# Attention scores in one group of 512 columns a head, left-over keys on the whole array, scores kept in DRAM

## The chip, the core and the metric

The kernel runs on one core of a Trainium2 chip. A core has five engines that run side by side, each taking its own instructions in order: TensorE (PE; its weight loads are the row PEld), VectorE (DVE), ScalarE (ACT), GpSimd (POOL) and SyncE (SP, which here only issues DMAs). TensorE writes PSUM, eight banks of 2 KB a partition; everything else works on SBUF. The metric is the device time of one execution in microseconds. Of the kernel before there are three timed runs and one profiled execution.

## The reference

Attention that keeps the 32 largest scores of each row, then a mixture of experts in which each token goes to one expert. Batch 8, 8 heads, 576 positions, head size 64; 4608 tokens of 512 features, 8 experts with 1024 hidden units; all fp32.

```python
scores = scale * np.matmul(q, k.transpose(0, 1, 3, 2))
kth = np.partition(scores, -top_k, axis=-1)[..., -top_k:-top_k + 1]
scores = np.where(scores >= kth, scores, -1000000000.0)
attn = np.exp(scores - np.max(scores, axis=-1, keepdims=True))
attn = attn / (np.sum(attn, axis=-1, keepdims=True) + 1e-09)
x = np.matmul(attn, v)                       # then (token, head * 64)
logits = x @ w_gate
expert_idx = np.argmax(logits, axis=1)       # one expert a token
out[mask] = gate_w[mask, None] * (np.maximum(x[mask] @ w1[e], 0.0) @ w2[e])
```

## The kernel before, in words

**Tiles and steps.** A head has 576 = 4 x 128 + 64 rows: four main tiles of 128 rows (`MAIN`) and 64 left-over rows (`LEFT`). Two heads make a pair `p`; batch `b` has four pairs. The attention runs in 144 steps, nine for each two pairs (`NT` = 9), so eighteen for a batch. A step (`grp(t)`, L333) takes two tiles, tile i of the first and of the second head of a pair; one step in nine takes the left-over rows of two pairs instead. So a step has 2 x 128 rows of 576 scores, kept side by side in one `sb` buffer of 2 x 576 columns (`EX[t]`, seven buffers), in the order main keys of the first, left-over keys of the first, left-over keys of the second, main keys of the second.

**One pass of the loop (L962).** Every engine's part of a step lies some passes behind the step before it in the chain. In pass t the program issues:

- scores of step t+3 (`scores`, L347) in two halves. A half is two matmuls of 288 columns, one a head, with 64 rows of weights each, so that the two lie in the two halves of the array; they write `ps` (two banks, one buffer), and `evac` (L366) copies 2 x 288 columns out on ACT. The second half uses the same `ps`. The first half stands at the start of the pass, the second after `av`.
- `softmax` of step t-2 (L397): for each of the two tiles ACT writes the sign of score minus threshold into `sg` and counts it, and POOL adds that to `sb` in place (L409).
- `exps` of step t-4 (L428): ACT takes exp of `tt`, the 1152 turned columns in PSUM, into `et`.
- `av` of step t-5 (L432): the left-over keys by a full-array matmul (L454), the main keys by 16 half-width instructions (L439), into `px`.
- `transp` of step t-3 (L411): subtracts the row maximum by four bf16 matmuls (L422) and turns `sb` by nine transposes (L425) into `tt`.
- top-k of step t (`topk`, L373) on VectorE: 21 MAX8 over chunks of the scores, then MAX8 and MATCH_REPLACE8 over the candidates.

**Jobs.** Smaller work runs between the steps as generators. `advance` (L850) moves each on when its banks are free and the pass's limits allow it; what it issues goes into queues `pq`, `aq`, `dq`, `gq` that are flushed at fixed places of the pass (`pq` stands between the first half of the scores and `av`). `j_prep` turns q and k of a pair. The turned k (`kt`, twelve buffers) stays until its batch is done. `j_sums` and `j_rows` make row sums and write finished rows to DRAM (`xs`, `lps`). `j_find`, `j_redo`, `j_patch` mend up to 128 rows of a batch whose count of kept scores isn't 32: `j_find` fetches their q rows from DRAM, spreads them by head (`qx`, 512 columns) and turns them; `j_redo` forms their scores anew against the turned k of all heads, 2 x 4 matmuls of 288 columns, and finds the exact threshold; `j_patch` writes the mended rows. `j_route` gives each token its place. Loads of the next q and k (`load_qk`, L99) and v (L270) are issued on SP at fixed steps, and wait until the one buffer of `rq` or `rk` has been read.

**PSUM.** `tt` has three banks, of which the columns from 1152 on (`SPOTS`) serve small results of jobs; `ps` has two, `px` one, and two banks (`pt`) go round among the jobs.

**After the attention**, the experts: for each of eight blocks of hidden units of an expert, `hidden` (L1102) and `project` (L1117) in split fp32r; the change doesn't touch them. The first experts' work begins while the last batches' jobs end.

Of the kernel before, what the change touches and what calls it, by code (L numbers as in the profile page):

```python
# [47 lines left out]
def attention_moe(ctx, tc, q, k, v, w_gate, w1, w2, out):  # L48
# [50 lines left out]
    def load_qk(n):  # L99
# [3 lines left out]
        lq = work.tile([LEFT, 4, D], F32, name="lq", bufs=1)  # L103
        lk = work.tile([LEFT, 4, D], F32, name="lk", bufs=1)
        LD[n] = (rq, rk, lq, lk)

        for g in ((slice(0, 2), slice(2, 4)) if n == 0 else (slice(0, 4),)):
            hs = slice(4 * hf + g.start, 4 * hf + g.stop)
            for t, src, l, eng in ((rq, q, lq, nc.sync), (rk, k, lk, nc.sync if n or g.start else nc.scalar)):
# [133 lines left out]
    VV, KT, SB, EX, ET, XT, PX = {}, {}, {}, [], {}, {}, {}  # L243
# [44 lines left out]
    three = psum.tile([128, 3 * 512], F32, name="tt")  # L288


    SPOTS = dict(left=(0, 128), stat=(128, 8), li=(136, 8), logit=(144, 16), rank=(160, KB * E))

    def spot(name):
        if not att_open[0]:
            pt = bank()
            return pt, lambda: release(pt)
        o, w = SPOTS[name]
        held[0] += 1

        def leave():  # L300
            held[0] -= 1
            cell[0] += name == "left"
        return three[:, NB9 * 128 + o:NB9 * 128 + o + w], leave

    def j_prep(p):
        rq, rk, lq, lk = LD[p // 2]
        qt = QT[p % 3]
        hs = slice(2 * (p % 2), 2 * (p % 2) + 2)
        yield need(bank=1, pe=0.5, act=0.5)
        KT[p] = jobs.tile([128, KW], F32, name="kt", bufs=12)  # L310
        for r, d, o in ((rq, qt, 2 * LEFT), (rk, KT[p], LEFT)):
# [16 lines left out]
        act(nc.scalar.activation, kl, pt[:, None, LEFT:2 * LEFT].to_broadcast([128, 2, LEFT]), AF.Copy)
# [16 lines left out]
    EV = []  # L345

    def scores(slot, hf):  # L347
# [3 lines left out]
        if hf == 0:  # L351
            EX.append(pair())
# [1084 lines left out]
```

## Time and profile before

| | |
|---|---|
| median of 3 runs | 1362.01 us (1361.56 to 1364.34) |
| the profiled execution's own time | 1361.72 us |
| its span, first to last instruction | 1359.9 us |
| mean granted TensorE clock | 0.990 |
| busy, share of the span | PE 97%, DVE 76%, ACT 62%, POOL 67% |
| attention (steps and most jobs) | from about 7 to about 842 us |
| instructions | 32355 |
| DMA packets, bytes | 207878, 124.17 MB |

How to read the rows: in a timeline row stand the start in us, the length in us, engine, line, operation, output<-input tiles, partitions x columns, and the count of instructions merged into the row; a bracket tells the idle time before it and what ended it. A matmul's length is its way through the array, so the time from one start to the next tells what it costs in a row of matmuls. In a windows row stand the stretch, its length, each engine's busy time with its instructions, the granted clock, the DMA engines' busy share and GB/s. In a row of groups stand shape, count, busy us and mean ns. In a row of waits stand who waited for whom, us in total, times and the longest. fp32 matmuls run as two instructions each, transposes as one. L252 is the line of the helper that all jobs go through, so jobs are told apart by tile.

### The profile page before, as it was taken

How to read it: one execution, taken by the hardware profiler on the slowest of the kernel's cores; microseconds unless marked ns; L12 is line 12 of the kernel's file. 1: busy time of each engine (PE TensorE's matmuls, PEld its weight loads, DVE VectorE, ACT ScalarE, POOL GpSimd, SP SyncE). 2: the span in 40 equal slices, each digit the busy share in tenths (PEclk: the TensorE clock that was granted, in tenths of full speed). 3: DMA queues.
4: the chain of work that ended last, by engine and by line, in shares of the span. 5: the costliest groups of instructions: out<-in, count | busy, mean ns of one | idle time of the engine just before them, and what ended most of it. 6: DMA issues, size and time to landing. Idle time of an engine off the chain costs nothing.

```text
span 1359.9 us, 32355 instructions
## 1 busy us (share of the span) xinstructions
PE 1318.6 (97%) x10072; PEld 1037.0 (76%) x10072; DVE 1026.9 (76%) x6838; ACT 841.1 (62%) x1715; POOL 906.9 (67%) x1280
## 2 busy tenths in 40 slices
PE   6899999999999999999999998999999999999997
PEld 3667777777777777777777676888889899898996
DVE  7989998899999899999999795564674333345664
ACT  4888888788788789688788675333333233233432
POOL 4676877777787787787787797747654232355664
PEclk7999999999999999999999999999999999999999
DMA  4211312212212211221221022554665333346774
GB/s 117 56 37 42 77 36 57 61 42 58 61 41 57 62 42 50 59 51 42 61 57 42 16 63 69 158 171 136 187 174 158 97 124 94 112 139 185 218 217 127
DMA packets 207878, 124.17 MB, mean 91 GB/s; under 512 B 110104, under 2 KB 188104, under 8 KB 207696
## 3 DMA queue, kind: packets, MB, share of 16 engines
q1 hardware_dynamic: 197344, 100.95, 27.9%
q0 software_dynamic: 9120, 20.76, 4.9%
q8 instruction: 81, 1.33, 0.4%
q14 instruction: 101, 0.83, 0.2%
q10 hardware_dynamic: 1232, 0.30, 0.1%
HBM read 100.40 MB, written 22.96 MB: 91 GB/s over the span
## 4 chain that ended last, share of the span: by engine, by line
PE 88%; DVE 4%; issue 2%; ACT 2%; POOL 2%; DMA 1%; SPq 0%; another core or an unknown queue 0%; POOLq 0%; ACTq 0%; DVEq 0%
PE ph L1102 17%; PE y L1117 16%; PE ps L363 14%; PE pt L252 12%; PE px L439 10%; PE tt L425 9%; PE tt L422 6%; PE px L454 2%; DVE cand L983 2%; PE mt L1082 1%; PE tt L252 1%; POOL sb L409 1%; ACT sg L408 1%; DVE cand L989 1%; DVE vq L989 1%
## 5 line engine op out<-in xcount | busy, mean ns | idle before, releaser
L409 POOL TENSOR_TENSOR sb<-sb,sg 128x576 f32<-128x576 f32 x288 | 370.8, 1294 | 162.6 <-ACT sg L408 160.1
L983 DVE MAX8 cand<-sb 128x8 f32<-128x52 f32 (+2 forms) x3024 | 369.5, 207 | 6.4 <-ACT sb L368 3.7
L914 POOL TENSOR_TENSOR wl<-r,wh 128x512 fp32r<-128x512 f32 x110 | 143.0, 1300 | 217.2 <-DVE wh L913 211.9
L408 ACT ACTIVATE sg<-sb,nb 128x576 int8<-128x576 f32 x288 | 223.5, 776 | 41.7 <-POOL nb L985 39.3
L363 PE MATMUL ps<-kt,qt 64*128 64x288 f32 (+1 forms) x1152 | 237.9, 460 | 9.9 <-ACT sb L368 9.6
L368 ACT ACTIVATE sb<-ps 128x576 f32<-128x576 f32 x288 | 185.7, 645 | 99.1 <-PE ps L363 94.2
L1103 ACT ACTIVATE hh<-ph 128x320 fp32r<-128x320 f32 (+3 forms) x136 | 58.3, 428 | 242.5 <-PE ph L1102 212.8
L989 DVE MAX8 vq<-cand 128x8 f32<-128x22 f32 (+7 forms) x1152 | 202.3, 205 | 1.1 <-DVE cand L989 1.1
L1104 DVE SCALAR_TENSOR_TENSOR hl<-ph,hh 128x320 fp32r<-128x320 f32 (+3 forms) x136 | 65.0, 478 | 151.9 <-ACT hh L1103 134.1
L1102 PE MATMUL ph<-xh,wh 128*128 128x320 f32 (+3 forms) x536 | 168.4, 314 | 0.0
L439 PE MATMUL px<-et,rv 128*64 128x128 f32 (+1 forms) x2688 | 164.4, 266 | 3.3 <-issue 3.3
L425 PE MATMUL tt<-turner,sb 128*128 128x128 f32 x1296 | 167.0, 274 | 0.0
L430 ACT ACTIVATE et<-tt 128x1152 f32<-128x1152 f32 x144 | 161.8, 1124 | 7.8 <-remote 3.8
L1102 PE MATMUL ph<-xh,wl 128*128 128x320 f32 (+3 forms) x536 | 164.5, 307 | 0.0
L1102 PE MATMUL ph<-xl,wh 128*128 128x320 f32 (+3 forms) x536 | 164.3, 307 | 0.0
L989 DVE MATCH_REPLACE8 cand<-vq,cand 128x22 f32<-128x22 f32 (+2 forms) x864 | 157.3, 189 | 0.0
L363 PEld LDWEIGHTS ps<-kt,qt 64*128 64x128 f32 (+1 forms) x1152 | 101.7, 189 | 64.1 <-issue 31.1
L439 PEld LDWEIGHTS px<-et,rv 128*64 128x64 f32 x2688 | 130.5, 137 | 21.2 <-issue 4.7
L425 PEld LDWEIGHTS tt<-turner,sb 128*128 128x128 f32 x1296 | 140.3, 142 | 0.0
L1117 PE MATMUL y<-wh,hl 128*128 128x512 f32 x324 | 128.1, 395 | 0.0
L1117 PE MATMUL y<-wl,hh 128*128 128x512 f32 x324 | 128.0, 395 | 0.0
L1117 PE MATMUL y<-wh,hh 128*128 128x512 f32 x324 | 127.8, 394 | 0.0
(257 smaller groups left out, 2337.0 us busy)
## 6 DMA issues: line engine op xcount, KB each, us to landing
r<-in_moe_w_dram SPq DMA_DIRECT2D x220, 256.0 KB
rv<-in_v_dram SPq DMA_DIRECT2D x32, 256.0 KB
xs<-xm SPq DMA_DIRECT2D x16, 512.0 KB
rq<-in_q_dram SPq DMA_DIRECT2D x60, 128.0 KB
rk<-in_k_dram SPq DMA_DIRECT2D x60, 128.0 KB
rv<-in_v_dram SPq DMA_DIRECT2D x64, 32.0 KB
xs<-xl SPq DMA_DIRECT2D x32, 32.0 KB
lps<-lp SPq DMA_DIRECT2D x16, 64.0 KB
```

Source lines behind the costliest of these rows:

```text
L252: return lambda f, *a, **k: queue.append(lambda: f(*a, **k))
L363: nc.tensor.matmul(ps[:, n, 0:HALF], QT[p % 3][r, w], KT[p][r, o:o + HALF], start=True, stop=True)
L368: nc.scalar.activation(d, ps, AF.Copy)
L408: nc.scalar.activation(upper(SG[i]), SB[u], AF.Sign, bias=nb[:, i, 1:2], accum_out=CNT[b][:, 2 * lt + i:2 * lt + i + 1])
L409: nc.gpsimd.tensor_tensor(SB[u], SB[u], SG[i], op=OP.add)
L425: nc.tensor.matmul(tt[:, c], x[:, c * 128:(c + 1) * 128], ident, start=False, stop=c in (3, 7, 8), is_transpose=True)
L430: nc.scalar.activation(ET[t], three[:, 0:NB9 * 128].rearrange("p (c q) -> p c q", c=NB9), AF.Exp, scale=0.125)
L439: yield lambda kb=kb, blk=blk: nc.tensor.matmul(px[h * 64:(h + 1) * 64, c], block(rv, p % 2, kb if kb < MAIN else MAIN + n, h), et[:, blk, q],
L983: one[m][0](*one[m][1])
L989: f(*a)
L1102: nc.tensor.matmul(ph, a[:, c, :], x[:, c, s], start=(m == 0), stop=(m == len(seq) - 1))
L1117: nc.tensor.matmul(PY[u, t], a[:, s], x, start=(f == 0 and m == 0), stop=(f == FC - 1 and m == 2))
```

## The change

- **Scores.** `scores` is no longer split by columns: each tile's 512 main keys are one matmul of 512 columns (64 rows of weights, two at a time as before) into `MAINS`, two banks, copied by one ACT instruction of 2 x 512 columns. The left-over keys of both heads come from `scores_left`: one matmul of 128 columns on the whole array, against the left-over keys of the pair laid out block-diagonally, into `LEFTS`, copied by one ACT instruction of 128 columns. In the step of left-over rows there are two matmuls of 512 columns on the whole array and four of 64.
- **Order in the pass.** `exps` and the first half of `softmax` come first, then the jobs' TensorE work (`pq`), then `scores`, the second half of `softmax`, `av`, `scores_left`, `transp`.
- **Stores.** After `scores_left`, SP stores the step's scores to DRAM (`SCD[b]`): three DMAs a step (128 x 512, 128 x 64, 128 x 576 elements), six in the step of left-over rows, 8 x 8 x 576 x 576 x 4 bytes in all. POOL's add in place of that step must wait for them.
- **Flagged rows.** `j_find` fetches the 128 rows of scores from `SCD[b]` by one indirect DMA in place of their q rows; `qx`, its turning, the matmuls of `j_redo` and their copies go.
- **q and k.** The turned q and k of a pair lie in one tile `qk` (three buffers), the left-over q and k rows of a pair are loaded into the two halves of one tile `lqk` and turned by one 128 x 128 transpose instead of two of 64.
- **PSUM.** `tt` keeps 1152 columns; `MAINS` has two banks; one bank, `last_bank`, holds `PX` (256 columns, two steps of `av`), `LEFTS` (128) and `NOOK` (128, for the left-over transposes of jobs). Other small job results now need one of the two `pt` banks. `av` issues its main keys first and the full-array matmul last, and the copy out of `PX` is 256 columns after every second step instead of 512 after four.

In order on TensorE, one pass of the loop. Before, from the transposes of one step to the next ones; `rq` is a job's work:

```order
L425 MATMUL tt<-turner,sb 128x128 x9
L363 MATMUL ps<-kt,qt_218 128x288 x2
L252 MATMUL pt_236<-turner,rq 128x128 x4
L454 MATMUL px<-et,rv_228 128x128
L439 MATMUL px<-et,rv_228 64x128 x8
L363 MATMUL ps<-kt,qt_218 128x288 x2
L422 LDWEIGHTS nr
```

The same place in the changed kernel:

```order
L446 MATMUL tt<-turner,sb 128x128 x9
L252 MATMUL pt_236<-turner,rq 128x128 x4
L354 MATMUL ps<-qk_217 128x512 x2
L460 MATMUL px<-et,rv_227 64x128 x8
L475 MATMUL px<-et,rv_227 128x128
L367 MATMUL px<-qk_217 128x128
L443 LDWEIGHTS nr
```

The two score groups (L363) have become one (L354), the full-array matmul of `av` (L454, now L475) has moved behind the half-width ones, and the left-over scores (L367, shown under the bank's name `px`) stand between it and the row-maximum matmuls. So full-array work is now in one piece from L475 to the jobs.

In order on SP, around the load of the next q and k; `ll` is the reading back of logits for routing, `ntab` a table of `j_find`. Before:

```order
L753 DMA ll<-lps 128x256
L754 DMA ll<-lps 64x64
L111 DMA rq<-in_q_dram 128x4x64 x4
L112 DMA lq<-in_q_dram 64x4x64
L111 DMA rk<-in_k_dram 128x4x64 x4
L112 DMA lk<-in_k_dram 64x4x64
L580 DMA ntab_7133<-nb_222 128x74
```

After:

```order
L760 DMA ll<-lps 128x256
L761 DMA ll<-lps 64x64
L390 DMA sc_6620<-sb 128x512
L390 DMA sc_6620<-sb 128x64
L390 DMA sc_6620<-sb 128x576
L112 DMA rq<-in_q_dram 128x4x64 x4
L113 DMA lqk<-in_q_dram 64x4x64
L112 DMA rk<-in_k_dram 128x4x64 x4
L113 DMA lqk<-in_k_dram 64x4x64
L390 DMA sc_6620<-sb 128x512
L390 DMA sc_6620<-sb 128x64
L390 DMA sc_6620<-sb 128x576
```

Three stores of every step now stand between the loads, and each waits for ACT's copies of its step.

The core of the diff:

```diff
@@ load_qk
-        lq = work.tile([LEFT, 4, D], F32, name="lq", bufs=1)
-        lk = work.tile([LEFT, 4, D], F32, name="lk", bufs=1)
+        ll_ = work.tile([2 * LEFT, 4, D], F32, name="lqk", bufs=1)
@@ PSUM
-    three = psum.tile([128, 3 * 512], F32, name="tt")
+    three = psum.tile([128, NB9 * 128], F32, name="tt")
+    MAINS = psum.tile([128, 2, 512], F32, name="ps")
+    last_bank = psum.tile([128, 512], F32, name="px")
+    PX, LEFTS, NOOK = last_bank[:, 0:256], last_bank[:, 256:384], last_bank[:, 384:512]
@@ j_prep
-        for g, l in enumerate((lq, lk)):
-            pe(nc.tensor.transpose, pt[:, g * LEFT:(g + 1) * LEFT], l[:, hs, :].rearrange("p h d -> p (h d)"),
-               ident[0:LEFT, 0:LEFT])
+        pe(nc.tensor.transpose, pt[:, 0:2 * LEFT], lqk[:, hs, :].rearrange("p h d -> p (h d)"), ident)
@@ scores
-            o = (1 - n) * LEFT + hf * HALF
-            nc.tensor.matmul(ps[:, n, 0:HALF], QT[p % 3][r, w], KT[p][r, o:o + HALF], start=True, stop=True)
-        EV.append((EX[-1][:, :, hf * HALF:(hf + 1) * HALF], ps[:, :, 0:HALF]))
+            qk = QK[p % 3][r]
+            nc.tensor.matmul(MAINS[:, n], qk[:, 0, w], qk[:, 1, 2 * LEFT:], start=True, stop=True)
+        nc.scalar.activation(bass.AP(EX[-1].tensor, EX[-1].offset, [list(EX[-1].ap[0]), [S + LEFT, 2], [1, M]]), MAINS,
+                             AF.Copy)
+    def scores_left(slot):
...
+        if j < 2 * MAIN:
...
+            nc.tensor.matmul(LEFTS, qk[:, 0, 2 * LEFT + i * 128:2 * LEFT + (i + 1) * 128], qk[:, 1, 0:2 * LEFT],
+                             start=True, stop=True)
+        else:
+            for n in range(2):
+                qk = QK[(p + n) % 3]
+                for h in range(2):
+                    nc.tensor.matmul(LEFTS[:, n * LEFT:(n + 1) * LEFT], qk[:, 0, 0:2 * LEFT],
+                                     qk[:, 1, h * LEFT:(h + 1) * LEFT], start=(h == 0), stop=(h == 1))
+        nc.scalar.activation(EX[-1].rearrange("p a s -> p (a s)")[:, M:S + LEFT], LEFTS, AF.Copy)
...
+            for d, x in parts:
+                for dd, xx in ((d, x),) if n else ((d[:, LEFT:S], x[:, 0:M]), (d[:, 0:LEFT], x[:, M:S])):
+                    nc.sync.dma_start(dd, xx)
@@ j_find
-        qr = sm("r_qr", [128, D])
-        pool(nc.gpsimd.indirect_dma_start, out=qr, out_offset=None, in_=q.rearrange("b h s d -> (b h s) d"),
-             in_offset=bass.IndirectOffsetOnAxis(ap=qi[:, 0:1], axis=0))
+        sb = jobs.tile([128, S], F32, name="r_sb", bufs=2)
+        pool(nc.gpsimd.indirect_dma_start, out=sb, out_offset=None, in_=SCD[b],
+             in_offset=bass.IndirectOffsetOnAxis(ap=at[:, 0:1], axis=0))
...
-        pool(nc.gpsimd.tensor_tensor, qx, qr[:, None, :].to_broadcast([128, H, D]), hmb, op=OP.mult)
@@ j_redo
-            for hp in range(HP):
...
-                pe(nc.tensor.matmul, ps[:, 0:HALF], qt[:, hp * 128:(hp + 1) * 128], KT[b * HP + hp][:, c],
-                   start=(hp == 0), stop=(hp == HP - 1))
-            act(nc.scalar.activation, sb[:, c], ps[:, 0:HALF], AF.Copy)
@@ the loop
-        scores(grp(t + LA), 0)
-        flush(pq)
+        if grp(t - LAG - TD - 1):
+            exps(t - LAG - TD - 1)
         if grp(t - LAG):
             softmax(t - LAG, grp(t - LAG), 0)
-        evac()
-        if grp(t - LAG - TD - 1):
-            exps(t - LAG - TD - 1)
+        flush(pq)
+        scores(grp(t + LA))
...
-        scores(grp(t + LA), 1)
-        evac()
+        scores_left(grp(t + LA))
         if grp(t - LAG - TD):
             transp(t - LAG - TD)
```

More of the change, by code (lines that the diff above doesn't have):

```diff
@@ L301, in leave @@
             held[0] -= 1
-            cell[0] += name == "left"
-        return three[:, NB9 * 128 + o:NB9 * 128 + o + w], leave
+            cell[0] += 1
+        return NOOK, leave
     def j_prep(p):
-        rq, rk, lq, lk = LD[p // 2]
-        qt = QT[p % 3]
+        rq, rk, lqk = LD[p // 2]
+        qk = QK[p % 3]
         hs = slice(2 * (p % 2), 2 * (p % 2) + 2)
         yield need(bank=1, pe=0.5, act=0.5)
-        KT[p] = jobs.tile([128, KW], F32, name="kt", bufs=12)
-        for r, d, o in ((rq, qt, 2 * LEFT), (rk, KT[p], LEFT)):
+        for g, r in enumerate((rq, rk)):
             pt = bank()
@@ L429, in exps, with one @@
         ET[t] = work.tile([128, NB9, 128], F32, name="et")
-        nc.scalar.activation(ET[t], three[:, 0:NB9 * 128].rearrange("p (c q) -> p c q", c=NB9), AF.Exp, scale=0.125)
+        nc.scalar.activation(ET[t], three.rearrange("p (c q) -> p c q", c=NB9), AF.Exp, scale=0.125)
     def av(t, us):
         et = ET[t]
-        def one(px, c, p, h, n, q, main=False):
+        def one(px, p, h, n, q, kbs):
             rv = VV[p // 2]
-            for kb in range(MAIN if main else KB):
+            for kb in range(kbs):
                 blk = MAIN if kb == MAIN else n * (MAIN + 1) + kb
                 yield lambda kb=kb, blk=blk: nc.tensor.matmul(
-                    px[h * 64:(h + 1) * 64, c], block(rv, p % 2, kb if kb < MAIN else MAIN + n, h), et[:, blk, q],
-                    start=(kb == 0 and not main), stop=(kb == (MAIN - 1 if main else MAIN)))
+                    px[h * 64:(h + 1) * 64], block(rv, p % 2, kb if kb < MAIN else MAIN + n, h), et[:, blk, q],
+                    start=(kb == 0), stop=(kb == KB - 1))
         def both(a, b):
@@ L631, in j_find @@
         pool(nc.gpsimd.tensor_tensor, low, low, nb[:, 3:4], op=OP.add)
-        yield need(bank=1, pe=0.5, act=0.5, at=FREE)
-        FOUND[b] = (turn(qx, "r_qt"), nb, qi, hmb)
+        FOUND[b] = (sb, nb, qi, hmb)
     def turn(x, name, w=512):
@@ L648, in j_redo @@
             yield
[L649 removed]
+        sb, nb, qi, hmb = FOUND.pop(b)
         low = nb[:, 2:3]
[L651 to L661 removed]
+        yield need(slack=1)
+        yield need(act=0.8)
         wk = sm("r_wk", [128, S])
@@ L923, in ahead_take @@
         c, T = part_of[0]
-        GX[0] = [jobs.tile([128, KW], F32, name="kt", bufs=12)[:, 0:DM] for _ in range(T)]
+        GX[0] = [jobs.tile([128, DM], F32, name="kt", bufs=4)[:, 0:DM] for _ in range(T)]
         for i in range(T):
@@ L932, in ahead_split @@
                 SPARE.extend(t[:, c * DM:(c + 1) * DM] for c in range(2 * VW // DM))
-            SPARE.extend(jobs.tile([128, KW], F32, name="kt", bufs=12).bitcast(F32R)[:, 0:DM] for _ in range(2))
+            SPARE.extend(jobs.tile([128, DM], F32, name="kt", bufs=4).bitcast(F32R)[:, 0:DM] for _ in range(2))
         parts_w(k, [SPARE.pop(0) for _ in range(4)])
@@ L940, in attention_moe @@
     for t in range(LA):
-        for m in range(2):
-            scores(grp(t), m)
-            evac()
+        scores(grp(t))
+        scores_left(grp(t))
         for i in range(2):
```

95 lines of the change are left out of this document (44 added, 51 removed).

## The prediction

> **What bounds the kernel now.** I read the page's chain first, then busy time by stretch, then the timeline of one step, then the waits. The chain that ended last lies almost wholly on TensorE:
>
> ```profile
> PE 88%; DVE 4%; issue 2%; ACT 2%; POOL 2%; DMA 1%; SPq 0%; another core or an unknown queue 0%; POOLq 0%; ACTq 0%; DVEq 0%
> ```
>
> The attention I cut where VectorE begins the top-k of steps 9, 27, 45 and so on, so that each stretch holds the eighteen steps of one batch; the columns are the stretch, its length, then busy us of PE, PEld, DVE, ACT, POOL, the clock, the DMA share and GB/s. The last two rows lie ahead of the others in time:
>
> ```profile
> core 0: us, PE busy (x) PEld busy (x) DVE busy (x) ACT busy (x) POOL busy (x), PEclk, DMA share, GB/s
> 247.30:350.90 103.60, 103.56 (x931) 74.95 (x931) 95.86 (x795) 84.06 (x173) 80.48 (x116) 1.00 0.22 53
> 350.90:453.40 102.50, 101.65 (x897) 73.36 (x895) 94.86 (x795) 84.03 (x173) 80.95 (x119) 1.00 0.22 53
> 453.40:558.30 104.90, 104.00 (x931) 75.16 (x930) 96.06 (x796) 84.04 (x173) 83.22 (x122) 1.00 0.21 52
> 558.30:662.00 103.70, 102.80 (x915) 74.26 (x913) 96.24 (x796) 84.04 (x173) 82.07 (x121) 1.00 0.22 52
> 662.00:767.60 105.60, 101.55 (x897) 73.32 (x895) 95.35 (x796) 83.87 (x173) 83.70 (x125) 1.00 0.17 41
> 54.40:150.30 95.90, 93.82 (x871) 67.03 (x872) 88.10 (x764) 82.27 (x168) 67.92 (x91) 1.00 0.21 50
> 150.30:247.30 97.00, 97.00 (x863) 69.91 (x860) 91.10 (x780) 82.09 (x167) 71.05 (x98) 1.00 0.22 54
> ```
>
> In the five full batches a stretch takes 104.06 us in the mean, TensorE is busy for 102.71 of it and VectorE for 95.67 (92%); ACT and POOL have 20 us to spare. So TensorE bounds, and VectorE stands 8.4 us behind it: whatever TensorE is spared beyond 7 to 8 us a batch is worth nothing. VectorE's idle time is waiting for TensorE's and ACT's results:
>
> ```profile
> DVE xm L252 <- PE pt L252: 28.5, 17, 4.5
> DVE r_key L252 <- ACT sg L408: 22.4, 8, 4.6
> ```
>
> These two, 50.9 us in all, should go first when TensorE is faster, since `xm` waits for TensorE itself and `r_key` for the last step's sign.
>
> **TensorE, step by step.** One step without jobs, before:
>
> ```profile
> 403.23 0.76 PE L363 MATMUL ps<-kt,qt 64*128 64x288 f32 x4
> 403.92 0.66 PE L422 MATMUL tt<-identb,nr 128*128 128x512 bf16 x4
> 404.42 1.15 PE L425 MATMUL tt<-turner,sb 128*128 128x128 f32 x9
> 405.50 0.76 PE L363 MATMUL ps<-kt,qt 64*128 64x288 f32 x4
> 406.19 0.49 PE L454 MATMUL px<-et,rv 128*128 128x128 f32 x2
> 406.61 1.09 PE L439 MATMUL px<-et,rv 128*64 128x128 f32 x16
> 407.63 0.76 PE L363 MATMUL ps<-kt,qt 64*128 64x288 f32 x4
> ```
>
> From start to start: 0.69 + 0.50 + 1.08 + 0.69 + 0.42 + 1.02 = 4.40 us, no gap. What one instruction costs is seen where the same shape runs on the whole array (the step of left-over rows):
>
> ```profile
> 415.02 1.14 PE L363 MATMUL ps<-kt,qt 128*128 128x288 f32 x4
> 415.99 0.60 PE L252 MATMUL pt<-turner,rq 128*128 128x128 f32 x4
> 416.43 0.39 PE L454 MATMUL px<-et,rv 128*128 128x128 f32 x2
> ...
> 417.77 1.24 PE L363 MATMUL ps<-kt,qt 128*128 128x288 f32 x4
> 418.84 0.65 PE L422 MATMUL tt<-identb,nr 128*128 128x512 bf16 x4
> ```
>
> 288 columns cost 0.97 / 4 = 0.243 us, 128 columns 0.44 / 4 = 0.11, so 0.83 ns a column, and 512 columns 0.43. Four half-array matmuls of 288, two at a time, should cost 0.49 and cost 0.69; two full ones of 128 in L454 should cost 0.22 and cost 0.42. So each change of the array's shape costs about 0.2 us; the run L422 and L425 shows less, 0.50 + 1.08 against 0.48 (1152 bf16 columns at half the fp32 price) + 0.98, that is 0.12.
>
> A step now has five such runs, half, full, columns, half, full. After the change it has three: MAINS 2 x 0.43 + 0.20 = 1.06; `av` on the main keys 1.02; then L475, LEFTS, row maximum and transposes in one full run, 0.22 + 0.22 + 1.58 + 0.05 (between no more switching and 0.08 more) = 2.07. Sum 4.15, a gain of 0.25 although 64 more columns are computed; with the bounds of the switch, 0.2 to 0.3. Jobs in `pq` are full-array work and move from beside L454 to beside the transposes, a full run both times.
>
> The step whose `av` is that of left-over rows has no L454 to lose:
>
> ```profile
> 411.52 1.39 PE L439 MATMUL px<-et,rv 128*64 128x64 f32 x40
> ...
> 412.84 0.30 PEld L363 LDWEIGHTS ps<-kt,qt 64*128 64x128 f32 x4
> ```
>
> Before 2 x 0.69 + 1.32 + 1.58 = 4.28, after 1.06 + 1.32 + 0.22 + 1.63 = 4.23: 0.05. The step that scores left-over rows loses: 0.97 + 1.07 = 2.04 becomes 4 x 0.43 + 8 x 0.11 = 2.60 (a 64-column matmul isn't in the trace with such weights; between 0.055 by columns and 0.11 as for 128, I take 0.11, since each loads 128 columns of weights). Nine steps: 7 x 0.25 + 0.05 - 0.56 = 1.24; a batch 2.5 us.
>
> **Flagged rows.** The matmuls of `j_redo` and the turning of `qx` go:
>
> ```profile
> L252 PE MATMUL pt<-kt,r_qt 128*128 128x288 f32 x128 | 34.5, 412 | 0.0
> L252 PE MATMUL pt<-turner,r_qx 128*128 128x128 f32 x32 | 5.2, 285 | 0.0
> ```
>
> 128 x 0.243 + 32 x 0.11 = 34.6 us, 4.3 a batch. The last batch's lie after the attention, on the chain:
>
> ```profile
> 876.16 1.94 PE pt L252 x8
> 880.91 1.94 PE pt L252 x8
> ```
>
> 3.9 + 0.4 = 4.3 us off the end, if nothing else is late there. POOL's spreading and three ACT copies go too; neither bounds.
>
> **Left-over transposes.** In a step with them:
>
> ```profile
> 421.10 0.66 PE L252 MATMUL pt<-turner,rk 128*128 128x128 f32 x4
> 421.68 0.27 PE L252 MATMUL tt<-turner,lq 64*128 64x64 f32 x1
> 421.80 0.22 PE L252 MATMUL tt<-turner,lk 64*128 64x64 f32 x1
> 421.95 0.49 PE L454 MATMUL px<-et,rv 128*128 128x128 f32 x2
> 422.37 1.09 PE L439 MATMUL px<-et,rv 128*64 128x128 f32 x16
> ```
>
> 1.27 us from `rk` to L439 become 0.44 + 0.11 + 0.22 + 0.20 = 0.97: 0.3 a pair, 1.2 a batch.
>
> TensorE thus loses 2.5 + 4.3 + 1.2 = 8.0 us a batch and comes to 94.7, VectorE stays at 95.7: the bound passes to VectorE, with TensorE close behind. ACT copies the same 1152 columns a step in two instructions both times, and `px` in smaller pieces; its 20 us hide that.
>
> **New waits.** SP's three stores wait for ACT's copy of LEFTS; behind them on SP stand the loads of q, k and v, the rows' stores and `ll`. POOL's add in place waits for stores that were issued five passes before, over 20 us. Now the loads run ahead, and first use is far:
>
> ```profile
> 390.63 2.19 SPq L111 DMA_DIRECT2D rq<-in_q_dram x4
> ```
>
> Issued at 390.63, they are used at 415.99 (row above). After the change they are issued after their pass's stores, at the end of the fourth pass ahead of that use: about 9 us later, and ten loads at 0.55 us (2.19 / 4) are out 6 us after. That leaves about 10 us, so I charge nothing. The queues:
>
> ```profile
> q1 hardware_dynamic: 197344, 100.95, 27.9%
> ```
>
> By bytes the 84.9 MB of stores take 84.9 / 100.95 x 27.9% x 1360 us = 319 us of the 16 engines' time; over some 800 us of attention the share rises from 0.21 to about 0.6. The experts' stretch carries 0.52 beside a full TensorE:
>
> ```profile
> 900.00:1100.00 200.00, 199.04 (x1077) 178.49 (x1076) 108.06 (x229) 66.80 (x133) 103.21 (x128) 1.00 0.52 147
> ```
>
> so I charge nothing here either.
>
> **The sum.** How near two engines at 94.7 and 95.7 come to being both full isn't in the trace. TensorE alone at the bound reached 93.82 / 95.90 = 98% in the earliest stretch and 99% in the five; VectorE is at 92%. I take 97%, nearest to the first: a batch takes 95.67 / 0.97 = 98.6, 5.4 less, five times 27. From 150 to 247: 91.10 / 0.97 = 93.9, 3.1 less. From 54 to 150 (no flagged rows yet): TensorE 93.82 - 3.7 = 90.1, over 0.97 is 92.9, 3.0 less. The nine steps after 767: 2.7. The end: 4.3. The first 54 us, the fill: 0. In all 40 us, 1361.7 - 40 = 1321 us, against a profiled execution that lies 0.3 us under the median of the runs shown. With 100% the gain is 62 (1300).
>
> **Rivals.** *VectorE keeps waiting.* It works in order, and a job's result that comes a pass later stops its top-k however fast TensorE is; the two wait rows speak for it, that both waits are on what gets faster speaks against. At 94%, half-way between 92 and 97, a batch takes 101.8 and the gain is 11 + 0 + 0 + 1 + 4 = 16: 1345.
>
> *The shared bank.* `PX`, `LEFTS` and `NOOK` lie in one bank. In the trace an ACT copy already waits for matmuls that write other columns of its bank:
>
> ```profile
> ACT qt L252 <- PE tt L425: 9.6, 23, 0.4
> ```
>
> So each `av` will have to wait for ACT's copies of LEFTS and PX of the step before. The Trainium skill, PSUM — Partial Sum Buffer, section "PSUM bank collisions raise a hardware error", says that two engines must be kept apart by bank and quadrant and not by address, and this row agrees. ACT copies LEFTS some 1.5 us (row maximum and transposes) before the next step begins, and `av` comes 1.06 later, so a busy ACT queue of over 2.5 us is needed to stop it; if it cost 0.28 us in each of 144 steps, all 40 us would be gone: 1361, no change.
>
> *SP is late (slower).* The waits of SP are long now, with nothing behind them:
>
> ```profile
> SPq L753 <- DMA lps<-r_lr,r_qi: 123.7, 8, 19.8
> SPq L111 <- PE pt L252: 104.6, 9, 30.8
> ```
>
> If stores and loads queue behind them, TensorE's transposes of the next q and k stand still. It decides from 10 us of delay; at 14 us, each of 14 rounds of loads costs 4: 1321 + 56 = 1377. Against it: these are waits of an SP that came early; with a store of every pass ahead of them it comes when what they wait for is done.
>
> **How the numbers follow.** Forecast 0.66, VectorE keeps waiting 0.18, shared bank 0.06, SP late 0.10. The range reaches from full overlap, 1300, to past the first rival, 1350; the last two lie outside. About 0.2% (2.7 us) is what a measurement of this kernel can tell from no change. Faster 0.84, same 0.06, slower 0.10.
>
> **What would show it.** Right: stretches of eighteen steps near 98 us with VectorE at 97%; PE rows with 1.06 us from L354 to L460 and the three-run step at 4.15; `DVE xm <- PE pt` nearly gone. Wrong: PE idle for ACT at `av` (shared bank), for DMA at the `rq` transposes or POOL for DMA at the add (SP late), or VectorE still at 92 to 94% with TensorE idle (first rival).

## The result and the profile after

The changed kernel takes 1327.3 us (median of 4 runs, 1325.86 to 1328.44), the kernel before 1362.99 beside it: a ratio of 0.9738, 95% interval 0.9721 to 0.9755. The profiled execution takes 1327.61 us, its span is 1325.8 instead of 1359.9: 34.1 us less.

The chain that ended last has left TensorE in part; VectorE now carries 19% of it where it carried 4%:

```profile
PE 62%; DVE 19%; issue 6%; POOL 5%; ACT 5%; DMA 2%; SPq 1%; POOLq 0%; ACTq 0%; DVEq 0%
```

Busy time by stretch, cut at the top-k of steps 9, 27, 45 and so on as before (columns as before; here in order of time):

```profile
56.10:146.60 90.50, 89.91 (x835) 65.37 (x831) 87.03 (x764) 80.97 (x167) 68.56 (x90) 1.00 0.61 179
146.60:236.90 90.30, 90.07 (x830) 66.25 (x827) 90.30 (x780) 78.61 (x163) 69.67 (x95) 1.00 0.57 172
236.90:337.90 101.00, 99.55 (x907) 73.62 (x905) 100.44 (x796) 85.33 (x178) 83.53 (x121) 1.00 0.58 168
337.90:435.80 97.90, 95.07 (x865) 70.27 (x864) 97.87 (x795) 81.76 (x171) 81.84 (x119) 1.00 0.58 169
435.80:533.80 98.00, 95.36 (x866) 70.42 (x866) 97.81 (x796) 81.95 (x171) 81.99 (x119) 1.00 0.58 165
533.80:631.70 97.90, 95.11 (x865) 70.23 (x864) 97.71 (x796) 81.81 (x171) 81.82 (x119) 1.00 0.57 168
631.70:733.80 102.10, 97.10 (x865) 70.96 (x864) 96.24 (x798) 81.65 (x171) 83.12 (x121) 0.98 0.52 155
```

In the three middle batches TensorE is busy for 95.2 us of 97.9 and VectorE for 97.8. So VectorE is full, and TensorE is idle for 2.7 us a batch. In the three together TensorE stands for 3.3 us with no wait that the profile shows (`issue`), waits 4.7 us for copies by ACT, and not once for VectorE. All its waits from 250 to 720 us:

```profile
PE px L460 <- issue: 4.2, 6, 1.2
PE px L460 <- ACT xt L252: 4.1, 5, 0.9
PE pt L252 <- ACT qk L252: 2.3, 1, 2.3
PE pt L252 <- ACT r_et L252: 2.2, 5, 0.4
PE pt L252 <- ACT po L252: 1.4, 5, 0.3
```

The stretches give 5.4 and 6.7 us (the two early ones) and 520.3 - 496.9 = 23.4 (the five full batches). Step 9 begins 1.7 us later than before (56.1 against 54.4), and from step 135 to the end it takes 592.0 us against 592.3. -1.7 + 5.4 + 6.7 + 23.4 + 0.3 = 34.1.

One step on TensorE, in the timeline:

```profile
399.91 1.13 PE L354 MATMUL ps<-qk 64*128 64x512 f32 x4
400.97 1.09 PE L460 MATMUL px<-et,rv 128*64 128x128 f32 x16
402.00 0.49 PE L475 MATMUL px<-et,rv 128*128 128x128 f32 x2
402.32 0.39 PE L367 MATMUL px<-qk 128*128 128x128 f32 x2
402.54 0.65 PE L443 MATMUL tt<-identb,nr 128*128 128x512 bf16 x4
403.03 1.16 PE L446 MATMUL tt<-turner,sb 128*128 128x128 f32 x9
404.03 0.17 PE L252 MATMUL pt<-r_ok,before 128*128 128x1 bf16 x1
```

From start to start 1.06 + 1.03 + 0.32 + 0.22 + 0.49 + 1.00 = 4.12 us. Of VectorE's waits over the attention (54 to 734 us), the two that the prediction named are down to 0.5 and 2.5 us; one of 5.0 us, for the routing (`skip`), stands near the end:

```profile
DVE skip L252 <- PE pt L252: 5.0, 1, 5.0
DVE r_key L252 <- ACT sg L429: 2.5, 1, 2.5
...
DVE xm L252 <- PE pt L252: 0.5, 1, 0.5
```

VectorE does the same instructions as before (795 or 796 a batch) in 2 us more. Where they went is seen where one small operation meets POOL's adds, VectorE's row first, then POOL's:

```profile
431.06 2.34 DVE L252 SCALAR_TENSOR_TENSOR r_fl<-r_li 128x1 int32<-128x1 f32 x1
```
```profile
430.86 2.51 POOL L430 TENSOR_TENSOR sb<-sb,sg 128x576 f32<-128x576 f32 x2
```

An operation on one column, which takes 0.14 us elsewhere in this run, stands for 2.34 us and ends as POOL's two adds end. In the batch from 337.9 us six operations of jobs (L252) take over 0.3 us more than the shortest of the same tile and shape, 5.9 us together; five of them end 0.02 to 0.06 us after one of POOL's adds, the sixth 0.2 us after another operation of POOL. In the batch from 350.9 us before there are three, 1.9 us together. The Trainium skill, SBUF — State Buffer, section "SBUF: two separate sides", says that VectorE and GpSimd share a pair of ports as an exclusive lock, held for a whole instruction, against VectorE operations with two SBUF inputs or in a fast mode; this trace agrees, with the addition that the waiting VectorE operation was not let in between POOL's two adds.

The queue of the stores carries 85 MB more, as reckoned, and SP's longest waits are now the stores' own:

```profile
q1 hardware_dynamic: 260320, 185.92, 48.3%
```
```profile
SPq L390 <- ACT sb L356: 186.9, 77, 5.0
```

**The fill.** SP's queue, and TensorE's wait that follows from it:

```profile
10.39 7.87 SPq L390 DMA_DIRECT2D sc<-sb  x9
...
23.17 2.04 SPq L112 DMA_DIRECT2D rq<-in_q_dram  x4
```
```profile
26.35 1.51 PE L252 MATMUL pt<-turner,rq 128*128 128x128 f32 x3 [7.80 <-DMA rq<-in_q_dram]
```

The nine stores of the first three steps stand ahead of the second load of q, which was issued at 14.77 us before and now at 23.17; TensorE stands still for 7.80 us.

**The end.** TensorE reaches the experts earlier and then waits for the gathered tokens (`gx`):

```profile
902.70 0.63 PE L1087 MATMUL mt<-turner,gx 128*128 128x128 f32 x4 [3.40 <-DMA gx<-xs,ids]
```

Marks in the traces tell where the end's gain went. The last instruction of `av` starts at 839.9 us before and 805.8 after, 34.0 earlier; the 40th `project` matmul after the first at 880.3 and 839.1, 41.2 earlier; the 400th at 1069.9 and 1035.8, 34.1 earlier. The 4.3 us of the last batch's matmuls, and more, were gained, and given back within the next 200 us.

### The profile page after: what moved, and what is told of

It reads as the page before. It is cut to its first block, busy times and chain, and to the rows that moved or that the text cites. A ratio compares the mean times of both kernels' runs of the same rounds, so it can differ in the third digit from the quotient of the medians.

```text
span 1325.8 us, 32793 instructions
## 1 busy us (share of the span) xinstructions
PE 1265.1 (95%) x9688; PEld 1007.6 (76%) x9688; DVE 1037.6 (78%) x6838; ACT 823.2 (62%) x1691; POOL 905.2 (68%) x1272
## 4 chain that ended last, share of the span: by engine, by line
PE 62%; DVE 19%; issue 6%; POOL 5%; ACT 5%; DMA 2%; SPq 1%; POOLq 0%; ACTq 0%; DVEq 0%
PE ph L1107 16%; PE y L1122 15%; DVE cand L988 9%; PE ps L354 6%; PE px L460 6%; PE pt L252 5%; PE tt L446 5%; DVE cand L994 3%; DVE vq L994 3%; PE tt L443 3%; PE px L475 2%; ACT sg L429 2%; POOL sb L430 2%; PE mt L1087 1%; PE px L367 1%
## 5 line engine op out<-in xcount | busy, mean ns | idle before, releaser
L460 PEld LDWEIGHTS px<-et,rv 128*64 128x64 f32 x2688 | 132.1, 138 | 122.6 <-issue 57.5
L994 DVE MAX8 vq<-cand 128x8 f32<-128x22 f32 (+7 forms) x1152 | 205.2, 207 | 0.8 <-DVE cand L994 0.8
L451 ACT ACTIVATE et<-tt 128x1152 f32<-128x1152 f32 x144 | 163.1, 1132 | 44.3 <-PE tt L446 43.5
L354 PE MATMUL ps<-qk 64*128 64x512 f32 (+1 forms) x576 | 183.9, 646 | 3.1 <-ACT sb L356 2.5
L460 PE MATMUL px<-et,rv 128*64 128x128 f32 (+1 forms) x2688 | 166.7, 268 | 14.8 <-ACT xt L252 4.7
L356 ACT ACTIVATE sb<-ps 128x1024 f32<-128x1024 f32 x144 | 147.0, 1020 | 51.1 <-PE ps L354 48.1
L446 PE MATMUL tt<-turner,sb 128*128 128x128 f32 x1296 | 166.5, 273 | 0.6 <-POOL sb L430 0.6
L446 PEld LDWEIGHTS tt<-turner,sb 128*128 128x128 f32 x1296 | 139.4, 141 | 1.0 <-POOL sb L430 1.0
L1107 PEld LDWEIGHTS ph<-xh,wh 128*128 128x128 f32 x536 | 101.2, 189 | 3.5 <-issue 0.6
```

Of the source, the lines that this page charges most:

```text
L354: nc.tensor.matmul(MAINS[:, n], qk[:, 0, w], qk[:, 1, 2 * LEFT:], start=True, stop=True)
L356: nc.scalar.activation(bass.AP(EX[-1].tensor, EX[-1].offset, [list(EX[-1].ap[0]), [S + LEFT, 2], [1, M]]), MAINS, AF.Copy)
L446: nc.tensor.matmul(tt[:, c], x[:, c * 128:(c + 1) * 128], ident, start=False, stop=c in (3, 7, 8), is_transpose=True)
L451: nc.scalar.activation(ET[t], three.rearrange("p (c q) -> p c q", c=NB9), AF.Exp, scale=0.125)
L460: yield lambda kb=kb, blk=blk: nc.tensor.matmul(px[h * 64:(h + 1) * 64], block(rv, p % 2, kb if kb < MAIN else MAIN + n, h), et[:, blk, q] ...
L994: f(*a)
```

## The experiments

The theory: TensorE is spared about 7.5 us a batch, and VectorE is then the bound, its time lengthened by waits for POOL; the fill lost to the stores on SP, the end to waits for `gx`. The rivals: stores and their transfers cost time all along; the shared PSUM bank holds TensorE up; the gain comes from one part alone. All kernels are variants of the changed one except the two that start from the kernel before. The marks are read from each trace (step 9: its top-k's start); ratios are to the kernel before on the same chip.

| kernel | median us | ratio (95%) | step 9 | last av | 400th project | span |
|---|---|---|---|---|---|---|
| before | 1358.8 to 1364.9 by chip | 1 | 54.4 | 839.9 | 1069.9 | 1359.9 |
| after | 1327.3 | 0.9738 (0.9721 to 0.9755) | 56.1 | 805.8 | 1035.8 | 1325.8 |
| rows_only | 1357.0 | 0.9953 (0.9937 to 0.9970) | 58.7 | 835.0 | 1067.6 | 1357.6 |
| rows_loads | 1348.2 | 0.9916 (0.9900 to 0.9933) | 54.4 | 822.8 | 1055.8 | 1345.8 |
| left_first | 1476.7 | 1.0837 (1.0819 to 1.0855) | 56.7 | 955.9 | 1187.0 | 1476.9 |
| left_first_tt | 1355.0 | 0.9941 (0.9921 to 0.9962) | 57.0 | 833.7 | 1063.5 | 1353.6 |
| few_stores | 1322.3 | 0.9702 (0.9685 to 0.9720) | 54.5 | 799.4 | 1033.1 | 1323.1 |
| pe_less | 1352.0 | 0.9927 (0.9904 to 0.9949) | 55.3 | 792.1 | 1024.3 | 1349.5 |
| fl_pool | 1329.3 | 0.9749 (0.9730 to 0.9768) | 55.1 | 802.6 | 1034.6 | 1324.6 |
| loads_first | 1319.0 | 0.9686 (0.9671 to 0.9702) | 54.3 | 797.6 | 1028.5 | 1318.4 |
| loads_fl | 1320.4 | 0.9689 (0.9673 to 0.9706) | 54.4 | 797.6 | 1024.6 | 1314.6 |
| tail_load | 1316.5 | 0.9688 (0.9674 to 0.9701) | 55.4 | 798.5 | 1024.4 | 1314.4 |
| loads_tail2 | 1320.9 | 0.9721 (0.9707 to 0.9734) | 54.5 | 799.5 | 1027.0 | 1317.0 |
| loads_order | 1312.8 | 0.9622 (0.9602 to 0.9643) | 53.8 | 797.9 | 1020.2 | 1310.2 |

### One part alone: stores and fetch of the flagged rows

On the kernel before: `j_find` fetches from the stored scores, `j_redo` has no matmuls, and the stores follow the second `evac`:

```diff
         scores(grp(t + LA), 1)
         evac()
+        store(grp(t + LA))
```

> The kernel before, with the stores of the scores and the fetch of the flagged rows alone; scores in two groups of 288 columns, order, PSUM and transposes as before. Theory (TensorE spared, then VectorE the bound): TensorE loses 4.3 us in each of seven batches, 102.7 to 98.4 a batch, still the bound at 99%, so about 99.5 a batch, 4.5 less; five batches 23, the stretch from 150 to 247 us 3, the first one 0, the end 0 to 4: 1362 - 28 = 1334 (1329 to 1340), with VectorE at 96 to 97%. Rival (the stores and their waits cost time): above 1345. Rival (the shape of the scores is what brought the gain): above 1350.

1357.0 us: 5 us less where 28 were expected, and so within what both rivals gave (above 1345, above 1350). On TensorE the batches did what the theory said; one of the middle ones:

```profile
353.90:454.30 100.40, 98.17 (x894) 70.83 (x893) 96.68 (x795) 82.43 (x171) 82.12 (x119) 1.00 0.57 163
```

TensorE 102.7 to 98.2 us a batch, 4.5 spared where 4.3 were reckoned, and four of the five batches take 100.3 in the mean, 3.4 less than the same four before. But the fill lost 4.3 us (step 9 at 58.7), the first batch 2.7 more (98.6 against 95.9 us), the last of the five 2.4 (108.0 against 105.6), and the end gave its gain back: from the last av to the 400th project matmul it takes 232.7 us where it took 230.1. The same with the first nine stores kept until the second loads are issued (`FIRST` collects them):

```diff
+    for dd, xx in FIRST:
+        nc.sync.dma_start(dd, xx)
     prep(2)
```

> The kernel before with stores and fetch of the flagged rows alone, and the nine stores of the first three steps behind the second loads of q and k. In the run without that, step 9's top-k began at 58.7 us instead of 54.4, and the first batch took 2.7 us longer. Theory (the stores cost in the fill, through SP, and there alone): 4 to 7 us come back, 1351 (1348 to 1354), step 9 at 54 us. Rival (the stores cost all along): 1356 to 1358.

Step 9 is back at 54.4 us and the time at 0.9916 instead of 0.9953. So the stores' cost lies in the fill for the most part, though this run also lacks the stops of TensorE told of in the last section. With the fill mended, the flagged rows alone bring 0.0084 of the time, some 11 us, and the whole change 0.0314, some 43 (`loads_first`, below): the other parts, shapes, order and transposes, bring about 31 of them. The rival that one part alone makes the gain falls.

### The stores left out

```diff
         b = p // HP
+        if b:
+            return
```

> The changed kernel with the scores of batch 0 alone stored; the flagged rows of every batch are fetched from batch 0's scores, positions and thresholds, so the mended rows of the seven other batches are not those of the reference. Theory (the stores cost nothing beyond the fill, which keeps them here): 1327, within 3 us, batches of 98 us with VectorE full, DMA share back near 0.2. Rival (stores slow other transfers, SP or POOL's add): 8 us or more faster, 1319 or less, with the gain in the batches after the first.

1322.3 us: 0.0036 of the time, 5 us, faster than the changed kernel, between the two expectations. What the mended rows hold also changes which tokens go where, so the experts are not compared; the attention's marks are: step 9 begins 1.6 us earlier, and a batch takes 97.5 us instead of 97.9:

```profile
330.70:428.20 97.50, 95.36 (x866) 70.38 (x864) 95.29 (x796) 81.82 (x171) 80.79 (x119) 1.00 0.23 59
```

VectorE's busy time has fallen by 2.5 us to 95.3, and the batch by 0.4 only. Here the small operations met POOL's adds less often (3.1 us by the same count). So VectorE's 97.8 us was not work that held the batch up. Nor do the stores and their transfers cost much all along, as the rival had it.

### Who bounds: VectorE or TensorE relieved alone

`r_fl` on POOL instead of VectorE:

```diff
-        vec(nc.vector.scalar_tensor_tensor, fl, li[:, 1:2], float(NLT + 1), li[:, 0:1], op0=OP.mult, op1=OP.add)
+        pool(nc.gpsimd.tensor_scalar, fl, li[:, 1:2], float(NLT + 1), li[:, 0:1], op0=OP.mult, op1=OP.add)
```

> The changed kernel with one small operation of j_find, r_fl, which takes 2.3 us on VectorE since it stands there until both of POOL's adds of its step have ended, moved to POOL itself. Theory (VectorE is the bound, and waits for POOL's adds are part of its busy time): VectorE 97.8 to 95.5 a batch; TensorE at 95.2 then stands as close, so a batch goes to 96.5 to 97.2 only: 1 us a batch, 1319 (1315 to 1324). Rival (VectorE alone bounds): 95.6 a batch, 1310. Rival (the wait moves on to the next such operation, or VectorE doesn't bound): 1327.

No change, as the rival said: 0.9749 beside 0.9738. VectorE has 3.6 us less in a batch and the batch 0.3:

```profile
331.80:429.40 97.60, 95.34 (x865) 70.34 (x864) 94.23 (x794) 81.73 (x171) 81.33 (x120) 1.00 0.57 169
```

TensorE with the full-array matmul of `av` left out (the left-over keys are missing):

```diff
-            nc.tensor.matmul(px, VV[p // 2][:, p % 2, o:o + 2 * D], et[:, MAIN, :], start=False, stop=True)
```

> The changed kernel without the full-array matmul of av (L475), so the left-over keys are missing from the result. TensorE is spared 0.22 us in sixteen steps of eighteen, 3.5 us a batch: 95.2 to 91.7. Theory (VectorE is the bound of the full batches): batches stay at 97.5 to 98 us with TensorE at 94%; only the two early stretches, where TensorE is as full as VectorE, and the catching up after the fill gain, some 4 us together: 1323 (1318 to 1327). Rival (TensorE, or the pair of them, still sets the time): a batch 94.5 to 95.5, 1302 (1298 to 1310).

The total, 1352.0, says nothing here: other values of x send other tokens to other experts, and TensorE waits 15.33 us in the last part, at 1321 us. The attention ends 13.7 us earlier (last av 792.1), of which some 7 have another cause, told in the last section (four stops of TensorE that this run doesn't show). A batch:

```profile
331.20:427.50 96.30, 92.22 (x833) 66.38 (x832) 96.27 (x796) 82.02 (x171) 82.14 (x119) 1.00 0.59 172
```

TensorE has 2.9 us less, VectorE is full, and the batch is 1.6 us shorter, about what the missing stops give. So relieving either engine alone moves the batch by 0 to 1.6 us.

The waits tell which engine held the other. With VectorE relieved (`fl_pool`), VectorE waits 10.1 us for ACT and TensorE in three batches (332 to 625 us), in the changed kernel hardly at all, and TensorE's idle times hardly change (6.9 us for 8.0): TensorE holds the batch. With TensorE relieved (`pe_less`), TensorE waits 5.3 us for VectorE in three batches (331 to 622 us), and VectorE is hardly idle: VectorE holds them, at 96.3, 96.4 and 98.1 us. The run `tail_load`, told of below and made on another chip, has the same instructions in these batches but not the stops, and takes 96.5 us, with VectorE at 95:

```profile
331.50:428.10 96.60, 94.67 (x865) 70.03 (x865) 94.59 (x795) 81.80 (x171) 81.24 (x119) 1.00 0.59 172
```

So in the changed kernel both engines are at a limit. TensorE's is 95.2 us of work and 2.7 of stops and waits for ACT, and it stays (97.6 in `fl_pool`) when VectorE is relieved. VectorE's is not fixed: with the same instructions it is busy for 94 to 98 us, by how often it meets POOL's adds. The theory that VectorE alone is the bound falls; the rival of the pair stands, though not its 94.5 to 95.5 us.

### The place of the left-over scores: the shared bank and the change of shape

`scores_left` right behind `scores`, ahead of `av`:

```diff
         scores(grp(t + LA))
+        scores_left(grp(t + LA))
...
-        scores_left(grp(t + LA))
```

> The changed kernel with the left-over scores put right behind the main-key scores, ahead of av, instead of behind it; nothing else. Theory (a change of the array's shape costs TensorE 0.2 us, and TensorE stands only 2.7 us a batch behind VectorE): two more changes a step, 0.4 us, 16 steps in 18, 6.4 us a batch: TensorE 95.2 to 101.6 a batch, the bound again, about 103: 4 to 5 us a batch more over eight batches, 1360 (1350 to 1368). The step from the scores to the scores at 4.5 us instead of 4.15. Rival (shape changes cost next to nothing, or VectorE hides them all): 1327 to 1330.

1476.7 us, 149 more than the changed kernel and far beyond both expectations. In the timeline of TensorE, one step:

```profile
440.58 0.49 PE L367 MATMUL px<-qk 128*128 128x128 f32 x2
442.65 1.81 PE L460 MATMUL px<-et,rv 128*64 128x128 f32 x16 [1.57 <-ACT sb L375]
```

And ACT at that place:

```profile
441.41 1.01 ACT L356 ACTIVATE sb<-ps 128x1024 f32<-128x1024 f32 x1
442.32 0.28 ACT L375 ACTIVATE sb<-px 128x128 f32<-128x128 f32 x1
```

`av` waits for ACT's copy of the left-over scores (L375): columns that `av` neither reads nor writes, but of the bank that it writes. ACT copies the main scores first. And after the wait the 16 instructions took 1.81 us instead of 1.09 (the granted clock was 0.97 in the stretch from 400 to 600 us, 1.00 in the changed kernel). The wait is one that the program sets, by a semaphore; what the chip would do without it no run here shows. The rival of the shared bank is real, then, and the order that the change chose, with row maximum, transposes and jobs between L367 and the next `av`, is what hides it. The same order with these scores in columns 1152 to 1280 of `tt`:

```diff
-    PX, LEFTS, NOOK = last_bank[:, 0:256], last_bank[:, 256:384], last_bank[:, 384:512]
+    PX, LEFTS, NOOK = last_bank[:, 0:256], three[:, NB9 * 128:NB9 * 128 + 128], last_bank[:, 384:512]
```

> The kernel of the run with the left-over scores right behind the main-key scores, whose av waited in every step for ACT's copy of them out of the shared bank; here they are written to columns 1152 to 1280 of tt instead, as jobs' results were before, so av has no copy to wait for. Theory (what cost 149 us was the shared bank's wait, and a change of shape costs 0.2 us): av's waits for ACT go, two changes of shape a step stay, TensorE 95.2 + 6.4 = 101.6 us a batch and full: 1360 (1350 to 1370). Rival (it was the change of shape, or the order of ACT's work): 1440 or more. Rival (changes of shape cost nothing): 1330.

1355.0: the wait that goes with the bank made 122 of the 149 us, and the changes of shape the rest of 28 at most. The step:

```profile
475.57 1.13 PE L354 MATMUL ps<-qk 64*128 64x512 f32 x4
476.63 0.49 PE L367 MATMUL tt<-qk 128*128 128x128 f32 x2
477.05 1.09 PE L460 MATMUL px<-et,rv 128*64 128x128 f32 x16
478.07 0.49 PE L475 MATMUL px<-et,rv 128*128 128x128 f32 x2
478.40 0.65 PE L443 MATMUL tt<-identb,nr 128*128 128x512 bf16 x4
```

L367 costs 0.42 us between half-width runs, and 0.22 in the run of the changed kernel; L460 and L475 cost what they cost there. So one excursion to the full array and back costs 0.20 us, not 0.20 at each end. A batch shows it: 98.15 us of TensorE, 3.0 more than the changed kernel (16 x 0.20 = 3.2), 100.50 us in all:

```profile
449.20:549.70 100.50, 98.15 (x866) 71.71 (x864) 95.52 (x796) 82.07 (x171) 81.23 (x119) 1.00 0.55 161
```

### The fill mended

On the changed kernel, the first nine stores behind the second loads (the edit shown with `FIRST`):

> The changed kernel with the nine stores of the first three steps issued behind the second load of q and k and the first load of v, not ahead of them. Theory (SP is late in the fill: TensorE waits 7.8 us for rq at 26 us, VectorE then 2.2 us): both waits go, step 9's top-k starts 2 us earlier, 54 instead of 56.1 us, and since VectorE is full from there on the whole kernel ends 2 us earlier: 1325.3 (1323.5 to 1326.5). Rival (the fill has slack, or the end waits for something else): 1327.3, no change.

1319.0, 0.9686: 8 us less, four times what was expected. The load of q is issued at 14.82 us again:

```profile
14.82 2.04 SPq L112 DMA_DIRECT2D rq<-in_q_dram  x4
```

Step 9 gains 1.8 us, and the first batch 3.9 more, 86.6 us instead of 90.5:

```profile
54.30:140.90 86.60, 85.72 (x804) 62.57 (x801) 86.42 (x764) 77.20 (x158) 65.64 (x87) 1.00 0.61 184
```

Of the 7.8 us that TensorE stood still, 7.4 of span come back. The expectation took VectorE for the bound and so counted its 2 us alone. TensorE carries its delay through the attention: its transposes (L446, here L451) of step 9 start at 80.7 us in the changed kernel and at 71.9 here, those of step 117 at 656.3 and 648.5. VectorE runs ahead of TensorE, and its marks show the whole delay only after the third batch (step 63 at 337.9 us there, 330.0 here). With `r_fl` on POOL as well:

> Both edits that leave the result whole: the first nine stores behind the second loads, and r_fl on POOL. Theory: their gains add, 8.4 us of the first and some 8 of the second: 1311 (1306 to 1317). Rival (they share one gain, VectorE's fullness): 1318, the first alone.

1320.4, 0.9689: nothing added, as `r_fl` alone.

### The end

TensorE work of the removed size put back into the last batch:

```diff
+        for hf in range(2 if b == B - 1 else 0):
+            yield need(bank=1, pe=2.0, at=FREE)
+            ps = bank()
+            for hp in range(HP):
+                pe(nc.tensor.matmul, ps[:, 0:288], ident, turner.rearrange("p a x -> p (a x)")[:, 0:288],
+                   start=(hp == 0), stop=(hp == HP - 1))
```

> The changed kernel with TensorE work of the size of the removed matmuls (2 x 4 of 288 columns and a copy of 288 columns on ACT after each four, on constants, the result used nowhere) put into the last batch's j_redo. Theory (the end is set by the last batches' routing, which reaches TensorE as a wait for gx, so the 4 us spared there were worth nothing): TensorE's waits for gx shrink from 3.4 and 1.7 us and the time stays: 1327 (1325.5 to 1329). Rival (TensorE's work sets the end): 1331.

1316.5, and 0.9688 where the changed kernel has 0.9738: faster with work added, below both expectations. Seven us lie in the attention (last av at 798.5), most of them from the stops of TensorE that this run doesn't have (last section). The end is what was asked for: from the last av to the 40th project matmul it takes 4.6 us longer than in the changed kernel (37.9 against 33.3), as the work added; yet from the last av to the 400th it takes 225.9 us against 230.0. The waits for `gx` are gone but for 0.5 us. So the work was worth nothing, and something that came with it was worth 4: the two `yield`s, by which the last batch's jobs move two turns later. In POOL's queue of the changed kernel:

```profile
891.78 0.98 POOL L1128 DMA_INDIRECT out_dram<-yo,ids  x1
...
893.07 0.98 POOL L746 DMA_INDIRECT lps<-r_lr,r_qi  x1 [0.24 <-issue]
...
897.10 0.98 POOL L841 DMA_INDIRECT gx<-xs,ids  x1 [0.18 <-issue]
```

The last batch's scatter (`lps`) stands ahead of `gx`; in the kernel before it stands behind it, `gx` at 937.18 and `lps` at 943.89. Moving the jobs on faster was tried first, with `TAIL = 2` on the kernel with the mended fill:

> The changed kernel with the first nine stores behind the second loads, and jobs moved on twice a pass instead of once in the five passes after the last step. Theory (the chain of the last batches' jobs sets the end): routing comes earlier, TensorE's waits behind the last av shrink, 1316 (1313 to 1319). Rival (the chain is bound by its own operations on POOL, VectorE and ACT, not by when they are issued): 1319, no change.

1320.9, 0.9721, beside 0.9686: no gain in all, though this run lacks TensorE's stops too. Its trace shows two changes that work against each other. The scatter is issued at 867.59 us, 23 us ahead of `gx` (890.63) and no longer just ahead of it, and from the 40th to the 400th project matmul it takes 189.1 us instead of 197.8; but from the last av to the 40th it takes 38.4 instead of 33.1, of which TensorE waits 5.9 us for ACT (`wh`). Then the two turns alone, without work:

```diff
+        for hf in range(2 if b == B - 1 else 0):
+            yield need(bank=1, pe=2.0, at=FREE)
```

> The changed kernel with the first nine stores behind the second loads, and the last batch's j_redo held back by two turns of the jobs, as many as the removed matmuls took, with no work in them; so POOL issues the gathers of tokens for the experts (gx) ahead of the last batch's scatter of mended rows, as in the kernel before, and not behind it. Theory (the end's gain was lost because fewer turns put POOL's scatters ahead of gx): TensorE's waits for gx, 3.5 and 1.1 us in the run without this, go, and from the last av to the 400th matmul of project it takes 226 us instead of 231: 1314 (1311 to 1317) beside a kernel before of 1362, a ratio of 0.9650. Rival (the order on POOL is beside the point, and the run with added work owed its time to something else): 1319, a ratio of 0.9686, waits as before.

1312.8 us, 0.9622: the fastest of all. POOL's queue and TensorE at `gx`:

```profile
882.21 0.98 POOL L1137 DMA_INDIRECT out_dram<-yo,ids  x1 [0.23 <-issue]
...
887.56 1.23 POOL L848 DMA_INDIRECT gx<-xs,ids  x1 [0.15 <-issue]
...
892.82 1.01 POOL L753 DMA_INDIRECT lps<-r_lr,r_qi  x1 [0.17 <-ACT xh L1097]
```
```profile
891.56 0.52 PE L1096 MATMUL mt<-turner,gx 128*128 128x128 f32 x3 [0.17 <-issue]
```

`gx` is issued as long after `out_dram` as in the changed kernel (5.3 us), but TensorE has it 4.0 us after the issue instead of 5.6 with the scatters ahead. From the last av to the 400th project matmul it takes 222.3 us, 230.9 with the fill mended alone: 8.6 us less where 5 were expected. Some 4 us are the waits for `gx`; in addition the granted clock was 0.94 from 880 to 910 us and 0.96 from 940 to 980 with the fill mended alone, and is 1.00 here.

The order on POOL parts all fourteen kernels. In the ten that issue the last batch's scatter 4 us ahead of `gx`, TensorE waits 3.9 to 5.7 us for `gx` between the 40th and the 400th project matmul, and that stretch takes 194.0 to 199.0 us. In the kernel before, `tail_load`, `loads_tail2` and `loads_order` it waits 0 to 0.8 us, and the stretch takes 188.0 to 189.6.

## Why the prediction was right where it was, and where it failed

The time was 6 us above the forecast and well inside the range; 34.1 of 40 us came. By its own steps:

- **"PE step 4.40 becomes 4.15".** Measured 4.12. The sum was right, in part by luck: L475 took 0.32 where 0.22 was reckoned, row maximum and transposes 0.49 + 1.00 where 1.63 was. Its unit was not right: "each change of the array's shape costs about 0.2 us" should be 0.20 for both changes of an excursion. It did no harm, since L454's excess of 0.2 was one excursion.
- **Flagged rows, 4.3 us a batch.** 4.5 in the run with that part alone. Step and transposes, 2.5 + 1.2 = 3.7: 3.0 (98.2 to 95.2). Together 7.5 of the 8.0.
- **"VectorE stays at 95.7" and "the bound passes to VectorE".** Failed. VectorE's busy time rose to 97.8, by waits for POOL's adds, which are longer and more frequent in the changed pass (5.9 us for 1.9 in one batch each), and with 94.2 the batch was the same. TensorE is still at its limit, with its stops and waits, and VectorE 0 to 1.6 us behind it. That a batch takes 1/0.97 of the bound's work came out (95.2 / 97.9 = 97%), but by luck: the 3% are TensorE's stops without a wait and its waits for ACT, for which the prediction has no term. The five batches were reckoned at 27 us and gave 23.4; the middle three at 97.9, 98.0, 97.9 were better than 98.6. The first was late from the fill (101.0, and 97.5 with the fill mended), the last holds VectorE's wait of 5.0 us for the routing (`skip`). The sum for 100% comes to 61 us by the terms given, not 62.
- **"The first 54 us, the fill: 0".** Failed, and it is the largest term that was missed: 7.4 us of span. The rival "SP is late" had the mechanism, with loads queued behind stores, and looked for it in the rounds of the steady state, where SP now comes in time; its first round, where nothing runs ahead, was not looked at.
- **The stores, charged nothing.** Some 5 us by the run without them, of which 1.6 are seen in the fill and 0.4 in each middle batch.
- **The end, 2.7 + 4.3 us.** Gave 0.3. TensorE was 41 us early at the 40th project matmul, so the work did come off; the condition, "if nothing else is late there", failed. With two waits of the generator gone, POOL's scatter of the last batch came ahead of the gathers for the experts. With the order mended, 8.6 us came back.
- **Shared bank.** Rightly small in this order; worth 122 us in another. The changed kernel still shows it a little: 4.1 us of TensorE's waits from 54 to 734 us are `av`'s for ACT's copy of `xt`.
- **"VectorE keeps waiting".** Its two wait rows came down from 43.5 us over the attention (54 to 768 us before) to 3.0 (54 to 734 us).

What stays open: why TensorE stops where it waits for nothing, and how far a batch would fall with both engines relieved. Sparing either by about 3 us did little; both at once wasn't tried.

## What to carry to other kernels

An engine's busy time is not its work: before calling a full engine the bound, look for operations that are long in one place and short in another, relieve it once, and see which engine waits then. An engine that is 3% idle can still be the bound, when what it waits for isn't the other engine. A removed step takes its turns in every hand-made order with it, so the queues that it passed through (here POOL's in the end, SP's in the fill) have to be read anew; both orders together were worth 0.0116 of the time, 16 us, against 36 for the change itself. And a layout that shares a PSUM bank between engines is as good as the order that keeps a copy away from the next write.

## What was not expected of the hardware

TensorE can stop with no semaphore waited for. In every second step of left-over rows from 342 to 636 us the 40 instructions of L460 took 3.1 to 3.2 us in the changed kernel, and 1.39 in `tail_load`, where the same instructions stand in the same order up to that place:

```profile
341.80 1.55 PE L460 MATMUL px<-et,rv 128*64 128x64 f32 x32
344.51 0.48 PE L460 MATMUL px<-et,rv 128*64 128x64 f32 x8 [1.16 <-issue]
```
```profile
340.18 1.39 PE L460 MATMUL px<-et,rv 128*64 128x64 f32 x40
```

Four such steps cost 7 us a run; the kernel before has them too (2.7 us in the same four). The kernels that ran beside `tail_load` on its chip (`rows_loads`, `loads_tail2`) had none either; of the others `pe_less` had none in these four steps, `rows_only` took 1.7 us in them, and `left_first` stopped in one. A late supply of instructions would look like this, but no run shows the cause; whether the chip or the place of the code decides wasn't tried. So kernels of different chips are compared here by ratios, and differences of 7 us between them only beside their traces.
